# One batch's transposes moved across an output stage, one batch's value load moved behind its transposes, and a gap between batches in the event pacing

## The chip, the cores and the metric

The kernel runs on one core of a Trainium2 chip. The metric is the device time of one execution in microseconds. TensorE (PE) multiplies, VectorE (DVE) and ScalarE (ACT) move and combine data between PSUM and SBUF, GpSimd (POOL) issues most loads, and SyncE (SP) issues the DMA transposes and half of the output stores. Each engine works through its own instructions in order and waits on semaphores.

## The reference

```python
# q, k, v: (8, 12, 448, 64) float32
scores = scale * np.matmul(q, k.transpose(0, 1, 3, 2))
attn = np.maximum(scores, 0.0) ** 2 / S
attn_out = np.matmul(attn, v)
x = attn_out.transpose(0, 2, 1, 3).reshape(B * S, H * D)     # (3584, 768)
gate = np.maximum(x @ w_gate, 0.0)                           # (3584, 1536)
val = x @ w_val
return gate * val @ w_out                                    # (3584, 768)
```

Attention with a squared ReLU in the place of the softmax is followed by a gated feed-forward network over all 3584 tokens. The result is float32; the kernel computes in bfloat16 with float32 sums.

## The kernel before

**Stages.** The loop `for b in range(1, B - 1)` (line 762) has six turns, called parts here. In part b, TensorE runs the gate and value projections of batch b-1 (twelve units, `gv_units`, each of twelve steps of four matmuls) and, woven between these steps, the attention of batch b and of batches after it. After parts 2 and 4 an output stage runs for two batches (`out_pair`, by a scheme of seven block products instead of eight, with sums of blocks made on DVE by `half_sums`, line 349, and adds at line 399). After part 6 come the projections and the output of the last two batches, outside of the loop.

**Events.** Work woven in is a list of events `(unit, step, function)`. `spread` (line 702) emits all events up to a place before the step at that place, so this list is the program order on every engine. A score tile (`scores_event`, `tile_of`, `relu2`) is four matmuls, a ReLU on ACT out of PSUM (line 232) and a square on DVE into `attn` (line 233). A values event (`values_event`, `values`) is 28 matmuls over seven score tiles, an evacuation on ACT and DVE (lines 266 and 267), and two copies between partition halves on DVE (line 261). At the end of a unit ACT makes `g_sb` (line 320) and DVE the product `hT` (line 321).

**Pacing.** From batch 4 on, the attention is one stream over four batches (`stream`), of which part 4 takes batch 4 and seven tiles of batch 5, part 5 the rest of batch 5 and fourteen tiles of batch 6, part 6 the rest. `paced` (line 740) lays the events of a part out over its steps in proportion to gaps between kinds of events. The batch is the first field of each event there.

**From a load to a tile.** For batches from 2 on, k and q go through one pair of buffers (`kn_b[0]`, `qn_b[0]`). `load_qk` and `load_v` issue DMAs from POOL (line 116). `regroup(b, t, h)` copies half of k (t = 0) or q (t = 1) on DVE into `kr` or `qr` (line 180). `transpose_grouped(b, t, h)` then issues two DMA transposes from SP into `T_b[b % 2]` (line 188), shown as `kqT`. `turned` (line 722) makes the four pieces of a batch into events, a regrouping and its transposes together; the halves of one piece are five steps apart, and the first place given is k's, the second q's. Score tiles of the batch read `T_b`. A tile needs the whole of q and a part of k.

**Holds.** `hold(b)` (line 688) makes POOL copy one element that the last transposes of batch b write, for k and for q; what POOL issues after it comes no earlier than these transposes' landing. `hold_unit(b, mf)` (line 684) does the same for one `hT` product.

**Where the work stands before.** In part 4, k and q of batch 5 have been issued in the part before; its values are issued at unit 0, step 4, its pieces stand at (2, 1) and (3, 1), then POOL holds for them and loads k and q of batch 6. Batch 6's pieces stand at (9, 6) and (10, 6). The output stage of batches 2 and 3 follows. In part 5, at (2, 1), POOL holds for a unit of batch 4, loads the values of batch 6, holds for batch 6's transposes, and loads k and q of batch 7, whose pieces stand at (7, 6) and (8, 6). The values event of batch 5 that ends part 4 stands at (11, 5).

Of the kernel before, what the change touches and what calls it, by code (L numbers as in the profile page):

```python
# [16 lines left out]
def kernel(  # L17
# [33 lines left out]
    NC = S // 64  # L51
# [16 lines left out]
    def pin(ins):  # L68
        return tc.keep_in_program_order(ins)
# [45 lines left out]
    def dma_in(o, i):  # L115
        pin(nc.gpsimd.dma_start(out=o, in_=i))  # L116
# [13 lines left out]
    def load_nat(dst, src, b, h0, h1):  # L130
        lo = src[b, h0:h1, 0:256, :].rearrange("h (j i) d -> j h i d", i=4)
        hi = src[b, h0:h1, 256:448, :].rearrange("h (j i) d -> j h i d", i=3)
        dma_in(dst[0:64, h0:h1, :, :], lo)
        dma_in(dst[64:128, h0:h1, 0:3, :], hi)

    def natural(b):

        return b if b < NB else 0

    def load_qk(b, h0=0, h1=H):  # L140
        load_nat(kn_b[natural(b)], k, b, h0, h1)
        load_nat(qn_b[natural(b)], q, b, h0, h1)

    def load_v(b):
        for c, p in HALVES:
            if b == 0:
                src = v[b].rearrange("(g c h) s d -> c h g s d", c=2, h=2)[c]
                dst = v_b[b % NB][p].rearrange("p (g h) i d -> p h g i d", h=2)
                parts = [(dst[:, h2], src[h2]) for h2 in range(2)]
            else:  # L150
                parts = [(v_b[b % NB][p], v[b, c * HP:c * HP + HP])]
            for dst, src in parts:
                dma_in(dst[:, :, 0:4, :], src[:, 0:256, :].rearrange("g (j i) d -> j g i d", i=4))
                dma_in(dst[:, :, 4:7, :], src[:, 256:448, :].rearrange("g (j i) d -> j g i d", i=3))
# [21 lines left out]
    def regroup(b, t, h):  # L176

        nat, grp = ((kn_b[natural(b)], kr), (qn_b[natural(b)], qr))[t]
        i = slice(2 * h, 2 * h + 2)
        pin(nc.vector.tensor_copy(grp.rearrange("p i (h d) -> p i h d", d=D)[:, i],  # L180
                                  nat.rearrange("p h i d -> p i h d")[:, i]))

    def transpose_grouped(b, t, h):

        grp = (kr, qr)[t]
        for i in (2 * h, 2 * h + 1):
            r = 128 if i < 3 else 64
            pin(nc.sync.dma_start_transpose(out=T_b[b % NB][:, t, :, i * 128:i * 128 + r], in_=grp[0:r, i, :]))
# [108 lines left out]
    def new_x(b):  # L297
        x = [xpool.tile([128, HP, S], BF16, name=f"x{n}") for n in range(2)]
        x_of[b] = [quads(t) for t in x]
        return x  # L300
# [284 lines left out]
    def gv_units(b):  # L585
        b0 = b - b % 2
        if b == b0:
            hT_of[b0] = hpool.tile([128, KF, 2 * S], BF16, name="hT")
        return [gv_unit(b, mf, BEGUN, rotation((BEGUN_IN[mf],))) if b == 0 and mf < len(BEGUN_IN) else
                gv_unit(b, mf, BEGUN if mf == 0 else STRAIGHT, acc) for mf in range(KF)]  # L590
# [85 lines left out]
    def values_event(b, qd):  # L676
        return lambda: (values_by_parity if b >= B - 2 else values)(b, qd, sc_later())

    def transposes_event(b, qd):
        return lambda: transpose_quad(b, qd)  # L680
# [3 lines left out]
    def hold_unit(b, mf):  # L684

        pin(nc.gpsimd.tensor_copy(flag[:, 2:3], hT_of[b - b % 2][:, mf, b % 2 * S:b % 2 * S + 1]))

    def hold(b):

        for t in range(2):  # L690
            pin(nc.gpsimd.tensor_copy(flag[:, t:t + 1], T_b[b % NB][:, t, HP - 1, S - 1:S]))  # L691
# [26 lines left out]
    def step(units, u, n, k):  # L718
        at = len(units[-1]) * u + n + k
        return at // len(units[-1]), at % len(units[-1])  # L720

    def turned(b, units, *at):

        def piece(t, h):
            regroup(b, t, h)
            transpose_grouped(b, t, h)
        return [(*step(units, u, n, 5 * h), lambda t=t, h=h: piece(t, h)) for t, (u, n) in enumerate(at) for h in range(2)]

    def stream(b0, b1):

        e = []
        for b in range(b0, b1):
            for n in range(NT):
                if n % NC == 2 and (b, n) != (b0, 2):
                    vb, qd = (b, n // NC - 1) if n > NC else (b - 1, NQ - 1)
                    e.append((b, n, values_event(vb, qd), NC))
                e.append((b, n, scores_event(b, n), 1))
        return e

    def paced(units, first, behind, events):  # L740

        at = [(u, n) for u in range(len(units)) for n in range(len(units[u]))][first:behind]
        gaps = [{(1, 1): 1, (1, NC): 0.35, (NC, 1): 0.75}[a[3], b[3]] for a, b in zip(events, events[1:])]
        gap = len(at) / (sum(gaps) + 1)
        places, due = [], gap / 2
        for (*_, e, _), g in zip(events, gaps + [0]):
            u, n = at[int(due)]
            places.append((u, n, e))
            due += g * gap
        return places  # L750
# [5 lines left out]
    units = gv_units(0)  # L756
# [5 lines left out]
    for b in range(1, B - 1):  # L762
        if b < B - 3:
            new_x(b)
        units = units[2:] if b == 1 else gv_units(b - 1)
        last = len(units) - 1
        if b < B - 4:
            first, behind = {1: (24, 105), 2: (40, 132)}.get(b, (0, 132))
            events = paced(units, first, behind, stream(b, b + 1))
            events.append((last, 8 if b == 1 else 5, values_event(b, NQ - 1)))  # L770
        else:
            todo = [e for e in attention if e[:2] <= ENDS[b]]
            del attention[:len(todo)]
            if b == B - 4:
                begun = flat(kn_b[1], 4, S)
                x_of[b + 1] = [[begun[:, 2 * e:2 * e + 2, :]] for e in range(2)]
                del attention[[e[3] for e in attention].index(NC)]
            events = paced(units, 0, 144 if b == B - 3 else 132, todo)
            if b != B - 3:
                events.append((last, 5, values_event(*((b + 1, 0) if b == B - 4 else (B - 1, NQ - 1)))))  # L780
        if b == 1:
            events += [(1, 2 + 4 * qd, transposes_event(1, qd)) for qd in range(NQ)]
            events += turned(2, units, (last - 3, 7), (last - 2, 7))
            events += [(last, 2, lambda: (hold(2), load_v(2), load_wo(), load_qk(3)))]
        elif b == 2:
            events += [(1, 1, lambda: load_v(3))]
            events += [(last - 5 + 2 * n, 6, lambda n=n: weight_sums(2 * n)) for n in range(2)]
            events += [(last - 1 + t, 3 + 5 * h, lambda t=t, h=h: regroup(3, t, h)) for t in range(2) for h in range(2)]
            events += [(last, 10, lambda: [transpose_grouped(3, t, h) for t in range(2) for h in range(2)])]
        elif b == 3:  # L790
            events += [(2, 1, lambda: (hold_unit(2, 1), hold(3), load_qk(4), load_v(4)))]
            events += turned(4, units, (6, 1), (7, 1)) + [(8, 4, lambda: (hold(4), load_qk(5)))]
        elif b == 4:
            events += [(0, 4, lambda: load_v(5))]
            events += turned(5, units, (2, 1), (3, 1)) + [(5, 4, lambda: (hold(5), load_qk(6)))]
            events += turned(6, units, (last - 2, 6), (last - 1, 6))
        elif b == 5:
            events += [(2, 1, lambda: (hold_unit(4, 1), load_v(6), hold(6), load_qk(7)))]
            events += turned(7, units, (last - 4, 6), (last - 3, 6))
            later = [xpool.tile([128, HP, S], BF16, name=f"x{n}") for n in range(2)]  # L800
            x_of[b] = [x_of[b][e] + quads(later[e])[1:] for e in range(2)]
            x_of[B - 2] = [quads(t)[:1] for t in later]
        elif b == 6:
            events += [(3, 1, lambda: (hold(7), load_v(7)))]
            new = [xpool.tile([128, HP, S], BF16, name=f"x{n}") for n in range(2)]
            x_of[b] = [x_of[b][e] + quads(new[e])[1:] for e in range(2)]
            x_of[B - 1] = [quads(flat(t, HP, S)) for t in (kr, qr)]
        spread(units, events)
        if b == 2:
            out_pair(0, flat(kn_b[1], KH, S), [lambda: weight_sums(1), lambda: weight_sums(3)])  # L810
        elif b == 4:
            out_pair(2, flat(v_b[0], KH, S))
# [48 lines left out]
```

## Time and profile before

| | |
|---|---|
| three runs, us | 401.11, 402.35, 404.22 |
| median, us | 402.35 |
| profiled execution: its own time, us | 403.33 |
| profiled execution: span of its instructions, us | 401.6 |
| PE busy, us (share of the span) | 389.9 (97%) |
| DVE busy, us | 302.9 (75%) |
| ACT busy, us | 243.6 (61%) |
| POOL busy, us | 96.3 (24%) |
| part 4, from its first step to the output stage | 160.3 to 200.6 us |
| output stage of batches 2 and 3 | 200.6 to 224.7 us |
| part 5 | 224.7 to 261.3 us |
| part 6 | 261.3 to 300.5 us |

All times in the profile count from the start of the span in the profiled execution. In the timelines a line gives the start, the length, the engine, the line of the kernel, the operation, what it writes and reads, how many instructions are merged, and in brackets how long the engine was idle before it and what ended that. In the windows view, each engine has its busy time and its number of instructions, and then come the granted clock of TensorE, the DMA engines' busy share and GB/s.

### The profile page before, as it was taken

The numbers are of one execution on the slowest core, as the hardware profiler recorded it, in microseconds if no ns is written. First come the engines' busy times: TensorE is split into PE (matmuls) and PEld (weight loads), VectorE is DVE, ScalarE is ACT, GpSimd is POOL, SyncE is SP. The second block draws the span as 40 slices with busy tenths as digits, with TensorE's granted clock in tenths as the row PEclk, the third lists the DMA queues.
The fourth block names the chain that finished last, engine by engine and source line by source line (L and its number), as shares of the span: only waits on it lengthen the run. The fifth ranks groups of instructions, "written<-read, shape, count | busy, mean of one in ns | idle before, by whom it ended". The sixth has DMA issues, their size and how long they took to land.

```text
span 401.6 us, 16574 instructions
## 1 busy us (share of the span) xinstructions
PE 389.9 (97%) x7376; PEld 290.5 (72%) x7376; DVE 302.9 (75%) x530; ACT 243.6 (61%) x358; POOL 96.3 (24%) x168
## 2 busy tenths in 40 slices
PE   7899999999999999999899999999999999999995
PEld 3466779978776666679677666988887766777664
DVE  4985896699944696887781478988889969997922
ACT  3962994787334776988533588899883234344231
POOL 7933300810213600503031360020003230000223
PEclk9999999999999999999999999999999999999999
DMA  9999998999836894997963588770002350000036
GB/s 151 168 196 197 196 191 97 155 205 179 135 83 179 108 163 82 149 154 86 171 110 80 160 108 103 122 89 4 4 2 52 77 153 3 2 3 3 20 83 177
DMA packets 90872, 44.17 MB, mean 110 GB/s; under 512 B 55424, under 2 KB 89792, under 8 KB 90800
## 3 DMA queue, kind: packets, MB, share of 16 engines
q0 software_dynamic: 51264, 28.83, 50.5%
q1 hardware_dynamic: 39104, 13.99, 19.8%
q8 instruction: 57, 0.93, 1.0%
q10 hardware_dynamic: 432, 0.30, 0.3%
q14 instruction: 15, 0.12, 0.1%
HBM read 47.19 MB, written 11.01 MB: 145 GB/s over the span
## 4 chain that ended last, share of the span: by engine, by line
PE 86%; DMA 5%; DVE 5%; issue 1%; ACT 1%; POOL 1%; ACTq 0%; DVEq 0%; POOLq 0%
PE ps L72 85%; DMA qn<-in_q_dram 5%; DVE attn L233 2%; ACT r_sb L232 1%; PE ps L208 1%; DVE kqT L209 1%; POOL kn L116 1%; POOL qn L116 0%; DVE x L267 0%; DVE hT L321 0%; DVE r_sb L630 0%; DVE x L653 0%; PE ps L217 0%; DVE x L261 0%; ACT g_sb L320 0%
## 5 line engine op out<-in xcount | busy, mean ns | idle before, releaser
L72 PE MATMUL ps<-x,gv 64*64 64x448 bf16 x3408 | 198.4, 349 | 1.2 <-DVE hT L321 0.9
L72 PEld LDWEIGHTS <-gv 64*64 64x64 bf16 x4032 | 150.5, 107 | 44.5 <-issue 2.9
L232 ACT ACTIVATE r_sb<-ps 128x896 bf16<-128x896 f32 x167 | 149.0, 933 | 17.7 <-PE ps L72 15.0
L233 DVE TENSOR_TENSOR attn<-r_sb 128x896 bf16<-128x896 bf16 x167 | 101.9, 622 | 29.2 <-ACT r_sb L232 22.0
L409 POOL DMA_DIRECT2D out_dram<-attn x63 | 33.1, 530 | 170.0 <-DVE attn L399 134.6
L72 PE MATMUL ps<-kqT 64*64 64x448 bf16 x672 | 68.6, 351 | 3.4 <-ACT r_sb L232 2.6
L72 PEld LDWEIGHTS <-hT 128*64 128x64 bf16 x1056 | 55.9, 110 | 20.9 <-issue 1.4
L395 ACT ACTIVATE attn<-ps 128x384 f32<-128x384 f32 (+1 forms) x64 | 28.8, 450 | 64.3 <-PE ps L72 63.3
L72 PE MATMUL ps<-wo,hT 128*64 128x384 bf16 (+1 forms) x720 | 54.3, 306 | 0.0
L321 DVE TENSOR_TENSOR hT<-ps,g_sb 128x448 bf16<-128x448 f32 x72 | 44.5, 619 | 8.3 <-ACT g_sb L320 7.5
L320 ACT ACTIVATE g_sb<-ps 128x448 bf16<-128x448 f32 x72 | 39.2, 546 | 17.3 <-PE ps L72 17.1
L399 DVE TENSOR_TENSOR attn<-ps,attn 128x384 f32<-128x384 f32 (+1 forms) x48 | 22.8, 503 | 33.0 <-ACT attn L395 18.4
L72 PEld LDWEIGHTS <-vn 64*64 64x64 bf16 (+1 forms) x888 | 35.8, 107 | 12.3 <-issue 2.3
L72 PEld LDWEIGHTS <-kqT 64*64 64x64 bf16 x672 | 28.3, 106 | 14.1 <-issue 6.0
L72 PE MATMUL ps<-attn,vn 64*64 64x448 bf16 x672 | 37.8, 350 | 0.7 <-DVE attn L233 0.7
L528 ACT ACTIVATE kqT<-ps 128x896 f32<-128x896 f32 x18 | 16.5, 918 | 25.0 <-PE ps L72 25.0
L116 POOL DMA_DIRECT2D vn<-in_v_dram x36 | 23.7, 678 | 17.8 <-PE ps L72 5.8
L72 PE MATMUL ps<-o_ring,hT 128*64 128x384 bf16 (+1 forms) x336 | 26.0, 306 | 0.0
L532 DVE TENSOR_TENSOR kqT<-ps,kqT 128x896 f32<-128x896 f32 x18 | 19.5, 1086 | 5.9 <-PE ps L72 4.2
L691 POOL COPY flag<-kqT 128x1 bf16<-128x1 bf16 x12 | 2.2, 197 | 89.7 <-DMA kqT<-kr 48.3
L116 POOL DMA_DIRECT2D qn<-in_q_dram x20 | 14.8, 762 | 1.3 <-POOLq L845 0.8
L261 DVE COPY x<-x 64x896 bf16<-64x896 bf16 x34 | 13.5, 397 | 1.8
(101 smaller groups left out, 288.5 us busy)
## 6 DMA issues: line engine op xcount, KB each, us to landing
out_dram<-attn POOLq DMA_DIRECT2D x48, 96.0 KB, 2.3
out_dram<-attn SPq DMA_DIRECT2D x48, 96.0 KB, 2.6
kn<-in_k_dram POOLq DMA_DIRECT2D x7, 384.0 KB, 6.8
qn<-in_q_dram POOLq DMA_DIRECT2D x7, 384.0 KB, 9.2
vn<-in_v_dram POOLq DMA_DIRECT2D x14, 192.0 KB, 8.8
gv<-in_moe_w_gate_dram POOLq DMA_DIRECT2D x6, 384.0 KB, 11.6
gv<-in_moe_w_val_dram POOLq DMA_DIRECT2D x6, 384.0 KB, 11.8
wo<-in_moe_w_out_dram POOLq DMA_DIRECT2D x2, 1152.0 KB, 13.7
```

The source lines that it names most:

```text
L72: pin(nc.tensor.matmul(o, lhsT=l, rhs=r, start=start, stop=stop, skip_group_check=True))
L116: pin(nc.gpsimd.dma_start(out=o, in_=i))
L232: pin(nc.scalar.activation(r, src, AF.Relu))
L233: pin(nc.vector.tensor_tensor(dst, r, r, ALU.mult))
L261: pin(nc.vector.tensor_copy(x1[p], x0[other]))
L320: pin(nc.scalar.activation(g_sb, o[0], AF.Relu, scale=float(out_scale)))
L321: pin(nc.vector.tensor_tensor(hT[:, mf, col:col + S], o[1], g_sb, ALU.mult))
L395: pin(nc.scalar.activation(out_of(t, r, c), bank(P, t), AF.Copy))
L399: pin(nc.vector.tensor_tensor(o, bank(Q, t), o, ALU.add))
L409: pin(engines[c].dma_start(out=rows[:, c0:c1, :], in_=src))
L528: pin(nc.scalar.activation(held(n, j), both(PQ[n][0]), AF.Copy))
L532: pin(nc.vector.tensor_tensor(k, both(PQ[n][1]), k, ALU.add))
```

## The change

In part 4, batch 5's pieces come one unit later, its values are loaded after the hold for its transposes and ahead of k and q of batch 6, and batch 6 is only regrouped, in the last two units; its eight DMA transposes are issued at the beginning of part 5, which in program order is behind the output stage. In part 5, the hold on a unit is gone, the hold for batch 6 comes ahead of its values, and this and batch 7's pieces stand later. In `paced`, the gap between two events of different batches is larger by one; only the streams of parts 4, 5 and 6 hold such a pair.

```diff
     def paced(units, first, behind, events):
 
         at = [(u, n) for u in range(len(units)) for n in range(len(units[u]))][first:behind]
-        gaps = [{(1, 1): 1, (1, NC): 0.35, (NC, 1): 0.75}[a[3], b[3]] for a, b in zip(events, events[1:])]
+        gaps = [{(1, 1): 1, (1, NC): 0.35, (NC, 1): 0.75}[a[3], b[3]] + (a[0] != b[0]) for a, b in zip(events, events[1:])]
         gap = len(at) / (sum(gaps) + 1)
...
         elif b == 4:
-            events += [(0, 4, lambda: load_v(5))]
-            events += turned(5, units, (2, 1), (3, 1)) + [(5, 4, lambda: (hold(5), load_qk(6)))]
-            events += turned(6, units, (last - 2, 6), (last - 1, 6))
+            events += turned(5, units, (3, 1), (4, 1)) + [(5, 4, lambda: (hold(5), load_v(5), load_qk(6)))]
+            events += [(last - 1 + t, 3 + 5 * h, lambda t=t, h=h: regroup(6, t, h)) for t in range(2) for h in range(2)]
         elif b == 5:
-            events += [(2, 1, lambda: (hold_unit(4, 1), load_v(6), hold(6), load_qk(7)))]
-            events += turned(7, units, (last - 4, 6), (last - 3, 6))
+            events += [(0, 0, lambda: [transpose_grouped(6, t, h) for t in range(2) for h in range(2)])]
+            events += [(3, 1, lambda: (hold(6), load_v(6), load_qk(7)))]
+            events += turned(7, units, (last - 3, 11), (last - 2, 11))
             later = [xpool.tile([128, HP, S], BF16, name=f"x{n}") for n in range(2)]
```

`last` is 11, the number of the last unit.

## Prediction, before the result

> **What bounds the kernel now.** I read the page first: TensorE (PE) is busy for 97% of the span, so only PE time counts. The windows view of the three parts that the edits touch comes next (part 4 is the one with b = 4, and so on):
>
> ```profile
> PE 389.9 (97%) x7376; PEld 290.5 (72%) x7376; DVE 302.9 (75%) x530; ACT 243.6 (61%) x358; POOL 96.3 (24%) x168
> ```
>
> ```profile
> 160.30:200.60 40.30, 38.50 (x800) 30.25 (x792) 32.07 (x60) 32.11 (x44) 9.00 (x14) 1.00 1.15 140
> 224.70:261.30 36.60, 36.60 (x776) 26.20 (x778) 29.43 (x54) 31.15 (x43) 7.42 (x14) 1.00 0.74 114
> 261.30:300.50 39.20, 39.20 (x833) 33.16 (x824) 33.72 (x60) 34.79 (x51) 2.83 (x5) 1.00 0.19 25
> ```
>
> The first figure after the stretch is its length, the second PE's busy time; the clock is 1.00 throughout. Now count the work. One step of a unit and one score tile are each one pass of four matmuls, and a values event is seven passes. Part 5 has 144 steps, 28 tiles and 3 values events: 193 passes in 36.6 us, 0.190 us each. Part 6 has 207 in 39.2 us, 0.189 us each. Part 4 has 200 and should take 37.9 us; it takes 40.3. So parts 5 and 6 are dense, and part 4 loses 2.4 us. That is all that these edits can win, 0.6% of the kernel.
>
> Where the 2.4 us go is in the timelines of PE and of VectorE (DVE):
>
> ```profile
> 194.22 0.95 PE L72 MATMUL ps<-x,gv 64*64 64x448 bf16 x14
> 196.03 1.13 PE L72 MATMUL ps<-x,gv 64*64 64x448 bf16 x18 [0.87 <-DVE hT L321]
> 196.82 1.48 PE L72 MATMUL ps<-attn,vn 64*64 64x448 bf16 x24
> 199.00 0.38 PE L72 MATMUL ps<-attn,vn 64*64 64x448 bf16 x4 [0.70 <-DVE attn L233]
> ```
>
> ```profile
> 193.88 0.56 DVE L180 COPY kr<-kn 128x1536 bf16<-128x1536 bf16 x1 [1.71 <-issue]
> ...
> 197.85 0.56 DVE L180 COPY qr<-qn 128x1536 bf16<-128x1536 bf16 x1 [0.81 <-issue]
> 198.33 0.62 DVE L233 TENSOR_TENSOR attn<-r_sb 128x896 bf16<-128x896 bf16 x1
> ```
>
> DVE works in order. At 193.88 and 197.85 it starts regrouping batch 6, and not before, because the loads of k and q land at 193.80 and 197.77; it reached these instructions at 191.4 and 194.7. A hT product and a square for attn are queued behind, and PE stands still for them twice, about 1.1 and 0.9 us beyond its pass time. The rest, some 0.4 us, is the same thing at 173.2, with q of batch 5 (landed 171.40). Why batch 6 is loaded so late stands in the timelines of GpSimd (POOL) and of SyncE (SP):
>
> ```profile
> 163.54 2.69 POOL L116 DMA_DIRECT2D vn<-in_v_dram  x4
> 180.62 0.19 POOL L691 COPY flag<-kqT 128x1 bf16<-128x1 bf16 x1 [14.40 <-DMA kqT<-kr]
> 186.03 0.20 POOL L691 COPY flag<-kqT 128x1 bf16<-128x1 bf16 x1 [5.22 <-DMA kqT<-qr]
> 186.54 1.50 POOL L116 DMA_DIRECT2D kn<-in_k_dram  x2 [0.32 <-DVE attn L233]
> ```
>
> ```profile
> 168.58 7.66 SPq L188 DMA_TRANSPOSE kqT<-kr  x4
> 176.76 7.93 SPq L188 DMA_TRANSPOSE kqT<-qr  x4
> 194.51 5.39 SPq L188 DMA_TRANSPOSE kqT<-kr  x4
> 199.99 6.14 SPq L188 DMA_TRANSPOSE kqT<-qr  x4
> ...
> 250.18 5.95 SPq L188 DMA_TRANSPOSE kqT<-kr  x4
> 256.22 6.05 SPq L188 DMA_TRANSPOSE kqT<-qr  x4
> ```
>
> The hold makes POOL wait until the eight transposes of batch 5 have landed, at 185.91. They took 17.3 us from the first issue, beside the values of batch 5, which landed between 172.4 and 176.7. The sets for batches 6 and 7 took 12.8 and 13.2 us.
>
> **The change, part by part.** Places are turned into times by the number of passes ahead of them, at 0.189 us, from 160.3 (part 4) and 224.7 (part 5).
>
> (1) *Batch 5's regrouping, one unit later.* The first copy moves from unit 2 to unit 3, step 1: 45 passes, 168.8; the hT product of unit 2 on DVE is ahead of it (its g_sb ran 169.1 to 169.6 on ScalarE, the product takes 0.62), so it runs at about 170.1 and SP issues the first transpose at 170.6. k has landed at 167.9. The q copy moves to unit 4 (67 passes, 173.0), after 171.4, so the stop at 173 goes: -0.4 us, inside the 2.4. The four copies (0.56 each) and eight transposes are the same in number.
>
> (2) *Values of batch 5 after the hold.* The transposes then have only the tail of q beside them. I take batch 7's 13.2 us: batch 5 done at 183.8 instead of 185.91. Bounds: 12.8 (batch 6) and 17.3 (nothing gained by the move); in between lies batch 4's 15.3, three us of it beside loads. PE's first tile of batch 5 stands at pass 137, 186.2, so this term is covered by 2.4 us.
>
> [...]
>
> (3) *The loads behind it.* From the last landing to the first issue 0.63 us pass (185.91 to 186.54): 184.4. Now comes the price: four issues for v stand ahead of k and q of batch 6. The nearest row is part 5 before, same order and nothing beside it: first issue 232.75, v landed 7.7 us later, k 11.2, q 15.0. So v at 192.2 (its values event at pass 186 begins at 195.5: covered), k at 195.7, q at 199.4. That is 1.9 and 1.6 us *later* than before, in spite of (2).
>
> (4) *Batch 6's regrouping, nine steps later.* k goes to unit 10, step 3 (170 passes, 192.5), q to unit 11, step 3 (184 passes, 195.1). DVE lags about 1 us behind; it waits for k some 2 us and for q about as long. What is queued behind is another set of work. Behind k's two copies: the squares of the last two score tiles, which the last pass of the values event needs. Copy 0.5, square 0.6, copy 0.5, square 0.6: the last pass starts 2.3 us after k lands. Before, 1.64 us lay between that pass (199.00) and the first product of the output stage (200.64), and 6.9 us from there to the first product that needs the sum S2 (207.5). So that product can start at k + 10.8 = 206.5. Behind q: copy 0.5, the evacuation of the values with its exchange 1.5, copy 0.5, last hT product 0.5, then six half sums of 0.77, the last of which is needed half a product (0.5) late; it can start at q + 7.3 = 206.7. PE without any stop would be there at 207.5 - 2.4 = 205.1. The last of the three counts: 206.7 against 207.5, **-0.8 us**. Before the change the same sums ended at 206.6, 0.9 before the need; that cover is gone.
>
> (5) *Transposes of batch 6 into part 5.* They stand on SP behind the output stores of batches 2 and 3 (last issue before: 226.78, 0.55 long), so first issue 227.4 - 0.8 = 226.6, done 13.2 later at 239.8. First need: the first tile of batch 6, pass 97, 223.9 + 18.4 = 242.3. Covered by 2.5 us: 0. Of this cover the new gap gives 0.4 (pass 97 instead of 95).
>
> (6) *Part 5's loads.* The hold on a unit goes (it kept POOL for 6.0 us, off the path); the hold for batch 6 now ends at 239.8. v first issued at 240.4, landed at 248.1 (need 253.1), k of batch 7 at 251.6, q at 255.4. The copies stand at passes 142 and 163, reached at about 251.8 and 255.8: covered by 0.2 and 0.4 only. Without that cover, a stop of DVE up to 2 us still leaves PE running, as the squares of the tiles that the values need are ahead of the first copy; in part 4 stops of 2.4 and 3.1 us cost PE 2.0. Taken at 0. Batch 7's transposes end near 266; its first tile in part 6 is at 270.
>
> (7) *The gap* moves score tiles by a few steps and adds no instruction: 0.
>
> Sum: -0.8 us on a span of 401.6, so 400.8; the profiled execution, 403.33, would be 402.5. The median of the runs shown is 402.35, 1.0 lower than that execution; less 0.8 it gives **401.6 us**. A measurement of this kernel can tell about 1% from no change, 4 us.
>
> **Rivals.** All turn on when a set of transposes ends; (3) and (4) give gain = 184.6 - (end of batch 5's set).
>
> *A, the loads come in time:* eight issues at 1.21 and a last landing after 2.3 (the shortest of the rows) make 12.0 us, 182.6, and 1.9 us gained, near the ceiling of 2.4. For it: no values beside the set. Against: every set seen had longer issues of about 2 us in it. Time 400.4.
>
> *B, slower: v in the queue ahead of q.* If batch 5's set takes over 14.0 us, the values placed in front push q of batch 6 beyond 199.9 and the output stage waits for its sums longer than all the stops of before. At batch 4's 15.3: +1.3 us, time 403.7; at 17.3, +3.3. For it: four of the six sets took 13.5 us or more, though with loads or stores beside them. Against: the two sets with least beside them. [...]
>
> *C, slower: batch 6's set behind the stores.* It decides from 15.7 us of length on, since PE then waits at pass 97 one for one, and the loads of batch 7 shift by as much. The set for batch 3, beside loads and stores, took 15.8; batch 5's 17.3 would cost 1.6: 403.2 with the rest as forecast.
>
> **How the numbers follow.** Forecast (0 to 1.4 us gained) 0.43, A 0.23, B 0.19, C 0.11, anything else 0.04. The likeliest gives 401.6; its own range is 400.9 to 402.4. Adding A down to the ceiling and B and C up to 17.3 gives gains of 2.4 to losses of 3.3 us, 400.0 to 405.7; the last us of the upper end needs the worst row, and the runs shown lie 3.1 apart, so I give 399.7 to 404.4. A gain of 4 us is beyond the ceiling: faster 0.03. A loss of 4 needs B and C together or what I don't see: 0.06. Within 1%: 0.91.
>
> **What would show it.** Right: no values load before 183 in part 4; batch 5's set in 13 us; batch 6's k and q landing near 195.7 and 199.4 and DVE still waiting at L180 for both; PE's wait now in front of the S2 products or of the last values pass; parts 5 and 6 as dense as before. Wrong: part 4 without a stop (A), S2 products after 207.5 (B), a PE wait on transposes in part 5 (C).

## The result and the profile after

The change makes the kernel slower: 407.81 us (median of 6 runs, 407.14 to 408.83) against 402.13 before, a ratio of 1.0124 with a 95% interval of 1.0100 to 1.0148. The forecast was 401.6. The profiled execution took 408.24 us, its span is 406.5 against 401.6. (Ratios here and below are made from undisturbed runs alone, which leaves out four of the twelve runs of e3, so they can differ from those of the medians.)

The windows view of PE, cut where PE's work changes; after each stretch its length, PE's busy time with the number of matmuls, the granted clock, the DMA share and GB/s:

```profile
160.40:196.50 36.10, 36.10 (x764) 1.00 0.88 121
196.50:199.60 3.10, 0.91 (x19) 1.00 1.38 173
199.60:203.00 3.40, 3.40 (x36) 0.50 0.04 4
203.00:226.40 23.40, 23.40 (x330) 1.00 0.34 86
226.40:254.00 27.60, 27.60 (x588) 1.00 0.79 121
254.00:264.00 10.00, 7.24 (x147) 1.00 1.20 161
264.00:305.90 41.90, 41.90 (x882) 1.00 0.28 37
```

Three places lose. At the end of part 4, PE is idle for 2.2 of 3.1 us. Then the granted clock is 0.50 for 3.4 us: in PE's timeline the last 28 matmuls of part 4 take 2.56 us, where they took 1.52, and the first 96 of the output stage 7.63, where they took 7.03. And part 5, dense before, is idle for 2.8 us of 10 near its end. (Parts 4 and 5 now begin at 160.4 and 226.4.)

The DVE timeline after, around batch 6's copies (L180, in part 4) and batch 7's (in part 5):

```profile
196.93 0.56 DVE L180 COPY kr<-kn 128x1536 bf16<-128x1536 bf16 x1 [2.99 <-DMA kn<-in_k_dram]
...
200.67 0.56 DVE L180 COPY qr<-qn 128x1536 bf16<-128x1536 bf16 x1 [1.10 <-issue]
...
257.96 0.56 DVE L180 COPY kr<-kn 128x1536 bf16<-128x1536 bf16 x1 [3.06 <-DMA kn<-in_k_dram]
258.44 0.62 DVE L321 TENSOR_TENSOR hT<-ps,g_sb 128x448 bf16<-128x448 f32 x1
...
262.53 0.56 DVE L180 COPY qr<-qn 128x1536 bf16<-128x1536 bf16 x1
```

The waits for batch 6 in part 4 have not gone (k landed at 196.85, q at 200.59, against 193.80 and 197.77), and there is a new one of 3.1 us for k of batch 7, whose q landed only at 261.47. Before, DVE came to the first copy of batch 7 without a wait:

```profile
249.56 0.56 DVE L180 COPY kr<-kn 128x1536 bf16<-128x1536 bf16 x1
```

PE's timeline after names what it waited for, first the squares behind batch 6's k, then what is queued behind batch 7's copies:

```profile
198.08 0.38 PE L72 MATMUL ps<-attn,vn 64*64 64x448 bf16 x4 [1.57 <-DVE attn L233]
199.08 0.38 PE L72 MATMUL ps<-attn,vn 64*64 64x448 bf16 x4 [0.62 <-DVE attn L233]
199.27 2.56 PE L72 MATMUL ps<-x,gv 64*64 64x448 bf16 x28
201.76 7.63 PE L72 MATMUL ps<-wo,hT 128*64 128x384 bf16 x96
...
259.11 0.38 PE L72 MATMUL ps<-x,gv 64*64 64x448 bf16 x2 [1.29 <-DVE hT L321]
261.83 0.38 PE L72 MATMUL ps<-kqT 64*64 64x448 bf16 x2 [1.20 <-DVE x L277]
```

The line before that answers to the 28 matmuls at half clock:

```profile
199.19 1.52 PE L72 MATMUL ps<-x,gv 64*64 64x448 bf16 x28
```

Why the loads are late stands in the timelines of SP and of POOL:

```profile
170.82 6.20 SPq L188 DMA_TRANSPOSE kqT<-kr  x4
177.54 6.32 SPq L188 DMA_TRANSPOSE kqT<-qr  x4
218.35 10.70 SPq L409 DMA_DIRECT2D out_dram<-attn  x16
229.15 6.46 SPq L188 DMA_TRANSPOSE kqT<-kr  x4
235.66 6.03 SPq L188 DMA_TRANSPOSE kqT<-qr  x4
```

```profile
185.75 1.32 POOL L116 DMA_DIRECT2D vn<-in_v_dram  x2 [0.33 <-issue]
187.54 1.32 POOL L116 DMA_DIRECT2D vn<-in_v_dram  x2 [0.47 <-issue]
188.84 1.53 POOL L116 DMA_DIRECT2D kn<-in_k_dram  x2
...
244.43 0.35 POOL L691 COPY flag<-kqT 128x1 bf16<-128x1 bf16 x1 [7.42 <-DMA kqT<-qr]
244.98 2.68 POOL L116 DMA_DIRECT2D vn<-in_v_dram  x4 [0.21 <-issue]
247.61 1.55 POOL L116 DMA_DIRECT2D kn<-in_k_dram  x2
```

In part 4, the values stand ahead of k and q. In part 5 everything is in a row: stores, batch 6's transposes (first issue 229.15, last landing 244.31), the hold, the values, then batch 7's k, issued at 247.61 where before it was 235.6.

In the spans: 1.7 us are lost up to the beginning of part 5 (226.4 against 224.7), 3.6 us in parts 5 and 6 (79.5 against 75.9), and the rest of the kernel takes 0.4 less, together the 4.9 us.

### The profile page after: what moved, and what is told of

Its sections match the earlier page's. It is cut to its first block, busy times and chain, and to the rows that moved or that the text cites. A ratio compares the mean times of both kernels' runs of the same rounds, so it can differ in the third digit from the quotient of the medians.

```text
span 406.5 us, 16576 instructions
## 1 busy us (share of the span) xinstructions
PE 391.7 (96%) x7376; PEld 275.9 (68%) x7376; DVE 303.6 (75%) x530; ACT 244.0 (60%) x358; POOL 96.6 (24%) x167
## 4 chain that ended last, share of the span: by engine, by line
PE 83%; DMA 7%; DVE 5%; issue 2%; POOL 1%; ACT 1%; SPq 0%; DVEq 0%; POOLq 0%; ACTq 0%
PE ps L72 82%; DMA qn<-in_q_dram 6%; DVE attn L233 2%; DMA kqT<-qr 1%; PE ps L208 1%; POOL vn L116 1%; ACT r_sb L232 1%; DVE hT L321 1%; DVE kqT L209 1%; POOL qn L116 0%; DVE r_sb L630 0%; DVE x L653 0%; DVE kr L180 0%; ACT x L276 0%; POOL kn L116 0%
## 5 line engine op out<-in xcount | busy, mean ns | idle before, releaser
L72 PEld LDWEIGHTS <-gv 64*64 64x64 bf16 x4032 | 139.5, 107 | 57.8 <-issue 4.5
L232 ACT ACTIVATE r_sb<-ps 128x896 bf16<-128x896 f32 x167 | 148.5, 933 | 20.6 <-PE ps L72 18.7
L233 DVE TENSOR_TENSOR attn<-r_sb 128x896 bf16<-128x896 bf16 x167 | 102.0, 622 | 30.5 <-ACT r_sb L232 24.7
L72 PE MATMUL ps<-kqT 64*64 64x448 bf16 x672 | 67.6, 351 | 4.3 <-ACT r_sb L232 2.6
L399 DVE TENSOR_TENSOR attn<-ps,attn 128x384 f32<-128x384 f32 (+1 forms) x48 | 22.8, 502 | 33.0 <-ACT attn L395 18.4
L72 PEld LDWEIGHTS <-vn 64*64 64x64 bf16 (+1 forms) x888 | 34.3, 107 | 15.4 <-issue 4.1
L72 PE MATMUL ps<-attn,vn 64*64 64x448 bf16 x672 | 37.7, 350 | 2.2 <-DVE attn L233 2.2
L72 PEld LDWEIGHTS <-kqT 64*64 64x64 bf16 x672 | 26.3, 106 | 16.8 <-issue 7.0
L528 ACT ACTIVATE kqT<-ps 128x896 f32<-128x896 f32 x18 | 16.5, 918 | 25.0 <-PE ps L72 25.0
L72 PE MATMUL ps<-kn,gv 64*64 64x448 bf16 x192 | 16.1, 349 | 0.0
L261 DVE COPY x<-x 64x896 bf16<-64x896 bf16 x34 | 14.4, 424 | 1.8
## 6 DMA issues: line engine op xcount, KB each, us to landing
gv<-in_moe_w_val_dram POOLq DMA_DIRECT2D x6, 384.0 KB, 12.2
```

Of the source, the lines that this page charges most:

```text
L72: pin(nc.tensor.matmul(o, lhsT=l, rhs=r, start=start, stop=stop, skip_group_check=True))
L232: pin(nc.scalar.activation(r, src, AF.Relu))
L233: pin(nc.vector.tensor_tensor(dst, r, r, ALU.mult))
L261: pin(nc.vector.tensor_copy(x1[p], x0[other]))
L399: pin(nc.vector.tensor_tensor(o, bank(Q, t), o, ALU.add))
L528: pin(nc.scalar.activation(held(n, j), both(PQ[n][0]), AF.Copy))
```

## The experiments

In this section "+x" is a time from the start of part 4 or of part 5 in the profile of that kernel, so that kernels can be compared. Times of runs are compared with the kernel before on the same chip, at 402.4 to 403.1 us.

**The pacing gap taken out** (e1).

```diff
-        gaps = [{...}[a[3], b[3]] + (a[0] != b[0]) for a, b in zip(events, events[1:])]
+        gaps = [{...}[a[3], b[3]] for a, b in zip(events, events[1:])]
```

> The change whole, but without the larger gap between batches in the pacing. Theory (late loads): the 5.7 us that the change cost come from VectorE waiting at L180 for batch 6's q in part 4 and for batch 7's k and q in part 5; the gap moves tiles by a few steps only. So 407 to 408 us, and the waits at L180 stay (about 3 us for batch 7's k in part 5). Rival (pacing): the gap squeezes the other events and stops PE; without it the time falls to 404 or less. A third possibility: without the gap the first tile of batch 6 stands two passes (0.4 us) earlier and PE waits for its transposes, 0.1 to 0.5 us more.

407.13 us, ratio 1.0102 (1.0073 to 1.0131): the loss stays, and the gap is not its cause. The profiled execution was the quickest of the six (405.30 us; the others took 406.92 to 408.79), so it is not typical, and it differed from the expectation: batch 6's transposes took 13.0 us instead of 15.2, batch 7's k landed at +28.7 instead of +31.5, VectorE waited 0.5 us for it and parts 5 and 6 lost 0.6 us only, while in part 4 PE's stop before the values was 2.8 us long. Two executions of nearly the same program, then, put the loss in different places. Of the 2.8 us by which k landed earlier in part 5, 2.2 are the shorter set of transposes; the loads behind it took 12.2 us to k instead of 12.9.

**Part 4 alone** (e2).

```diff
-            events += [(0, 4, lambda: load_v(5))]
-            events += turned(5, units, (2, 1), (3, 1)) + [(5, 4, lambda: (hold(5), load_qk(6)))]
-            events += turned(6, units, (last - 2, 6), (last - 1, 6))
+            events += turned(5, units, (3, 1), (4, 1)) + [(5, 4, lambda: (hold(5), load_v(5), load_qk(6)))]
+            events += turned(6, units, (last - 1, 3), (last, 3))
```

> The kernel before with the change's part 4 alone: batch 5's pieces a unit later, its values behind the hold, batch 6 regrouped in the last two units, but its transposes issued right with the regrouping, and part 5 and the pacing as before. Theory: batch 6's q lands near 200.6 as in the changed kernel, the products with S2 start 0.4 (at full clock) to 1.7 us later than before, part 5 loses nothing: 402.5 to 404. Rival (all of the loss is made in part 4 and only shows later): 406 or more.

404.75 us, ratio 1.0036 (1.0012 to 1.0060); parts 5 and 6 take 75.9 us as before. q of batch 6 lands at +40.2, as in the change, and the first product with S2 starts at +47.3, by the prediction's chain at +47.5 (before +47.2, in the change +48.8). The windows view of this kernel from the start of its output stage:

```profile
201.00:204.40 3.40, 3.40 (x52) 1.00 0.74 155
```

PE's stops before it were 1.39 and 0.62 us long, but the clock (the 1.00) stayed full. In these two profiles, then, the change's 1.5 us more at S2 are the half-clock stretch; the 28 and 96 matmuls above took 1.6 us longer in it.

The other executions of e2 are not all like the profiled one. For each the mean granted clock is on record, and one stretch of 3.4 us at half clock lowers it by 0.004 (half of 3.4 us in a span of some 404; the profiled execution of the change, with one stretch in its span, has 0.996). Five have 0.999 or 1.000 and took 401.95 to 404.23 us; seven have 0.993 or 0.996 and took 404.41 to 406.28. So e2's 404.75 holds half-clock stretches too, by these means, and the median of the five, 402.94, is close to the kernel before (402.66 on that chip). Where they lay is not on record, since only one execution was profiled.

**Part 5 alone** (e3, and e8 the same kernel again).

```diff
-            events += turned(6, units, (last - 2, 6), (last - 1, 6))
+            events += [(last - 2 + t, 6 + 5 * h, lambda t=t, h=h: regroup(6, t, h)) for t in range(2) for h in range(2)]
         elif b == 5:
-            events += [(2, 1, lambda: (hold_unit(4, 1), load_v(6), hold(6), load_qk(7)))]
-            events += turned(7, units, (last - 4, 6), (last - 3, 6))
+            events += [(0, 0, lambda: [transpose_grouped(6, t, h) for t in range(2) for h in range(2)])]
+            events += [(3, 1, lambda: (hold(6), load_v(6), load_qk(7)))]
+            events += turned(7, units, (last - 3, 11), (last - 2, 11))
```

> The kernel before with the change's part 5 alone: batch 6 regrouped where it was, its transposes at the beginning of part 5, then hold, values, k and q of batch 7, whose pieces stand later; pacing without the larger gap. Theory: part 5 loses about 3.3 us to VectorE's wait for batch 7's k and q, part 4 loses its 2.4 as before: 405 to 406. Rival (part 5's loss comes only because part 4 ended late): the chain from the stores to batch 7's k is tied to part 5's own start, so this would show as 402 to 403.

> The change's part 5 alone once more, since its runs fell into two groups, 399.2 to 401.0 and 403.6 to 406.3. Theory: batch 7's k is covered by a few tenths of a us, so that batch 6's set of transposes (13 to 15 us) and the loads (15 to 16.5 us) decide from run to run: two groups again, some 4 us apart. Rival (something of that chip): one group.

The first time 404.93 us (402.66 before), with four of the twelve runs at 399.2 to 401.0 and eight at 403.6 to 406.3, and a ratio that decides nothing (0.9986, 0.9946 to 1.0025), since it is made from four of each group. The second time there was one group, 403.9 to 406.8, median 404.8, ratio 1.0045 (1.0025 to 1.0065). Two groups were thus not reproduced, and what made the four quick runs is open: none of them was profiled. Both profiles show the loss: batch 6's set 15.0 and 16.0 us long, batch 7's k at +31.0 and +31.2, VectorE waiting for it for 2.4 and 1.9 us, parts 5 and 6 at 78.8 and 79.0 us instead of 75.9. Part 4 didn't end later than before (39.7 and 39.6 us against 40.3). So part 5's loss is its own. It is not all VectorE's: the first tile of batch 6 stands at +18.0 here, and it began 0.2 us after the set's last landing, 0.3 us late in e3 and 1.0 in e8. So PE seems to have waited for the set itself, though the profile names ACT as what ended these waits.

**Batch 7's pieces a unit later** (e4).

```diff
-            events += turned(7, units, (last - 3, 11), (last - 2, 11))
+            events += turned(7, units, (last - 2, 11), (last - 1, 11))
```

> The change whole, with batch 7's pieces one unit later still, at (9, 11) and (10, 11). Theory: k of batch 7 lands about 31.5 us after part 5's start, the copy is now reached at about 32, q lands at 35 and is reached at 34.5, so VectorE waits less than 1 us in all and PE gets back 2.5 to 3.3 us: 404.5 to 405.5. Rival (PE's stops in part 5 are not due to these copies): no change, 407 to 408.

404.8 us, ratio 1.0053 (1.0032 to 1.0074), as expected. k landed at +29.7 and was reached after that; VectorE doesn't wait at L180 in part 5, and parts 5 and 6 take 77.0 us. So 2.5 of the 3.6 us lost there are the meeting of late loads with early copies. The other 1.1 us have another cause, which is open: PE's only listed stop there is 0.2 us long.

**k and q of batch 7 ahead of the hold** (e5).

```diff
-            events += [(3, 1, lambda: (hold(6), load_v(6), load_qk(7)))]
+            events += [(3, 1, lambda: (load_qk(7), hold(6), load_v(6)))]
```

> The change whole, but in part 5 k and q of batch 7 are issued ahead of the hold for batch 6, the values of batch 6 behind it. Theory (serial chain: stores, batch 6's transposes, hold, values, then k and q): k and q of batch 7 now land before 250, VectorE doesn't wait at L180 in part 5, and the 3 us lost there come back, less what batch 6's transposes lose beside these loads (a set beside loads took 15 to 17 us, and PE's first tile of batch 6 stands 18.4 us after the part's start, the set begins some 3 us after it: 0 to 2 us lost): 404 to 406. Rival (it is the regrouping's place or the late transposes themselves): 407 or more.

410.71 us, ratio 1.0192 (1.0166 to 1.0217), slower than the change itself. The time falls into the rival's range, but by neither mechanism as I put it: VectorE no longer waits, while PE now stands before the first tile of batch 6. SP's timeline, and PE's from the list of its waits:

```profile
227.85 8.75 SPq L188 DMA_TRANSPOSE kqT<-kr  x4
236.65 10.11 SPq L188 DMA_TRANSPOSE kqT<-qr  x4
```

```profile
PE ps L72 <- DMA kqT<-qr: 3.7, 1, 3.7
PE ps L72 <- ACT r_sb L232: 1.2, 1, 1.2
```

Beside these loads the set took 20.7 us (+2.8 to +23.4), more than the 15 to 17 that I had expected, and the tile's place is +18.4. (The 1.2 us stop, some 2 us ahead of this tile, came with the edit too; its cause was not followed up.) After the stop of 3.7 us came 3.4 us at half clock again (249.5 to 252.9), and parts 5 and 6 took 83.3 us. With the transposes behind the output stage, the loads waited for them in the one order (k at +31.5), and in the other the set, beside the loads, was 5.5 us longer than in the change (20.7 us against 15.2).

**Batch 6's transposes back ahead of the output stage** (e9), the rest of the change kept.

```diff
-            events += [(last - 1 + t, 3 + 5 * h, lambda t=t, h=h: regroup(6, t, h)) for t in range(2) for h in range(2)]
+            events += turned(6, units, (last - 1, 3), (last, 3))
         elif b == 5:
-            events += [(0, 0, lambda: [transpose_grouped(6, t, h) for t in range(2) for h in range(2)])]
```

> The change whole, but batch 6's transposes issued right with its regrouping at the end of part 4, ahead of the output stage. Theory (part 5's loss comes from the place of these transposes behind the output stores): the hold in part 5 is over before it is reached, batch 7's k and q land before 255, VectorE doesn't wait for them, part 5 is dense; what is left is part 4's loss: 402.5 to 405. Rival (the later hold and the later pieces of batch 7 cost by themselves): 406.5 or more.

404.03 us, ratio 1.0052 (1.0023 to 1.0081). The set is over 15 us before part 5 begins, k of batch 7 lands at +12.8, and parts 5 and 6 take 76.3 us instead of 79.5. The place of the transposes is what costs in part 5.

**What costs in part 4.** Three kernels start from the one before and have batch 6's pieces at (10, 3) and (11, 3), with their transposes. They differ in batch 5's pieces and values:

```diff
-            events += turned(6, units, (last - 2, 6), (last - 1, 6))
+            events += turned(6, units, (last - 1, 3), (last, 3))
# e6: no more than this.  e10 besides:
-            events += [(0, 4, lambda: load_v(5))]
-            events += turned(5, units, (2, 1), (3, 1)) + [(5, 4, lambda: (hold(5), load_qk(6)))]
+            events += turned(5, units, (2, 1), (3, 1)) + [(5, 4, lambda: (hold(5), load_v(5), load_qk(6)))]
# e11 instead:
-            events += turned(5, units, (2, 1), (3, 1)) + [(5, 4, lambda: (hold(5), load_qk(6)))]
+            events += turned(5, units, (3, 1), (4, 1)) + [(5, 4, lambda: (hold(5), load_qk(6)))]
```

> The kernel before with one edit: batch 6's pieces nine steps later, at (10, 3) and (11, 3), transposes with them. Theory: k and q of batch 6 land at 193.8 and 197.8 as before, VectorE reaches them at 193.4 and 196.1, so it waits 0.4 and 1.7 us instead of 2.4 and 3.1, and the S2 products can start at 197.8 + 7.3 = 205.1, when PE gets there: 2 us faster than before, 400 to 401. Rival (the place of the regrouping is what costs in part 4 of the change): as slow as the kernel with the change's part 4 alone, 404 or more.

> The kernel before with batch 6's pieces at (10, 3) and (11, 3), as in e6, and batch 5's values behind the hold, batch 5's pieces at their old places. Tells apart what makes part 4 of the change slow. Theory 1 (batch 5's later pieces use up what its transposes gain without the values beside them): the set begins at 168.6, ends near 182.5, k and q of batch 6 land near 194 and 198: 400 to 401.5, as e6. Theory 2 (the values in front of k and q are the price): k and q land as late as in the change, 196.9 and 200.6: 403 to 405.

> The kernel before with batch 6's pieces at (10, 3) and (11, 3), and batch 5's pieces a unit later, its values at unit 0 as before: the other half of the change's part 4. Theory 1 (the later pieces cost): the set begins at 170.8 beside the values, ends at 186 to 188, k and q of batch 6 land at 194.5 and 198.5 or later: 400.5 to 402. Theory 2 (the values' place alone costs): as fast as e6, 400 to 401, with the set ending at 185 or before.

| kernel | batch 5's pieces | its values | its set of transposes | k, q of batch 6 landed | output stage from | time, us | ratio to before |
|---|---|---|---|---|---|---|---|
| before | unit 2 | early | +8.3 to +25.6, 17.3 us | +33.5, +37.5 | +40.3 | 402.1 (402.4 to 403.1 beside the others) | |
| e2 | unit 3 | behind hold | +10.6 to +24.5, 13.9 us | +36.3, +40.2 | +40.2 | 404.75 | 1.0036 (1.0012 to 1.0060) |
| e6 | unit 2 | early | +8.4 to +25.6, 17.2 us | +33.5, +37.7 | +38.4 | 400.62 | 0.9941 (0.9923 to 0.9959) |
| e10 | unit 2 | behind hold | +8.1 to +21.6, 13.5 us | +34.3, +37.9 | +38.7 | 401.84 | 0.9989 (0.9962 to 1.0017) |
| e11 | unit 3 | early | +10.6 to +24.7, 14.1 us | +32.8, +36.7 | +37.7 | 400.10 | 0.9941 (0.9919 to 0.9962) |

Regrouping batch 6 later, alone (e6), gains 2.4 us, as much as the prediction counted for part 4 (in its profile part 4 is 1.9 us shorter). Moving batch 5's pieces a unit later (e11) doesn't cost: its set, which runs beside the last 4 us of the values' loads where the set before ran beside 8, is 14.1 us long, the same as without them (14.3 in the change), and ends 0.9 us earlier than before. So in this pair the values' place alone costs: e2 and e11 differ in it only, and k and q land 3.5 us later in e2. That was theory 2. (Of the 4.65 us between their times a part is the half clock in seven of e2's executions.) Theory 1 has a share: with the pieces at their old place and the values behind the hold (e10), the set ends 4.0 us earlier, which pays for the values in front, and k and q land nearly as in e6. In time e10 stands between the two; its runs go from 400.3 to 405.1, and its interval includes no change (1.0). DVE still stops for batch 5's q there (1.4 us idle at 170.8).

PE in e11, part 4 first, then parts 5 and 6:

```profile
159.70:197.40 37.70, 37.70 (x802) 1.00 1.16 141
221.40:297.30 75.90, 75.90 (x1604) 1.00 0.47 68
```

Part 4 is dense, 37.7 us against 40.3: it beats both kernels.

**Batch 5's q later** (e7): e6 and

```diff
-            events += turned(5, units, (2, 1), (3, 1)) + [(5, 4, lambda: (hold(5), load_qk(6)))]
+            events += turned(5, units, (2, 1), (3, 6)) + [(5, 4, lambda: (hold(5), load_qk(6)))]
```

> As e6, and batch 5's q pieces five steps later, at (3, 6): VectorE then reaches them after q's landing at 171.4. Theory: 0.4 us more than e6, 399.7 to 400.7; SP is busy with k's transposes until 176 anyway, so batch 5's set ends no later. Rival: the set ends later by the five steps (1 us), the loads of batch 6 too, and the gain of e6 halves.

401.05 us, ratio 0.9950 (0.9932 to 0.9968), the same as e6 within the intervals. In the profile the stop at 173 is gone, PE has no other in part 4, and the set ends at +25.2, so the rival's price isn't paid; the 0.4 us don't show in the time.

## Why the prediction was wrong

*The ceiling* was right: the 2.4 us counted from passes are what e6 and e11 win. The prediction missed the span by 5.7 us (406.5 against 400.8): 2.5 up to the beginning of part 5, where it had 0.8 gained and 1.7 were lost, and 3.6 in parts 5 and 6, where it had none; the rest took 0.4 less.

*(1), batch 5's first transpose* at 170.6: it was 170.82.

*(2), its set*: 14.3 us instead of 13.2, ending at 185.11 instead of 183.8. By the prediction's own formula the 0.8 us gained become 0.5 lost. And its reason was only half of the story: e11 gets the same length by the later start, with the values' last 4 us beside it, e10 nearly the same (13.5) with the earlier start and no values beside it; one of the two edits is enough, and the change pays for both.

*(3) and (4), loads and chain*: right. From the first issue of the values k took 11.1 us and q 14.8 (11.2 and 15.0 forecast); the last values pass started 2.2 us after k (2.3); in e2 the S2 products came 0.2 us ahead of q + 7.3. This was rival B's side of the sum. What the prediction did not have is the half clock behind the stop: 1.5 us by the comparison of the two profiles of the change and e2.

*(5), batch 6's set in part 5*: first issue 2.7 us after the part's start, as forecast; 15.2 us long instead of 13.2. PE had no wait on it, but only 0.5 us of the 2.5 us of cover were left, so rival C did not come as described. In e8, with a set of 16.0 us and without the gap's 0.4 us, it seems to have come, at 1.0 us.

*(6) is the step that failed*, and it is the larger part of the miss. It had the copies covered by 0.2 and 0.4 us and took a stop of DVE behind that cover at nothing. The set was 2.0 us longer, and the loads behind it took 12.9 us to k and 16.5 to q instead of 11.2 and 15.0, so k landed at +31.5 instead of +27.7. DVE waited 3.1 us, where the prediction held up to 2 to be free, and parts 5 and 6 lost 3.6 us (2.8 of them as PE's idle time in that stretch); with a set of 13.0 us (e1) they lost 0.6, with the copies later (e4) 1.1, with the set ahead of the output stage (e9) 0.4. That up to 2 us should be free rested in part on a misreading: the "stops of 2.4 and 3.1 us" before, which cost PE 2.0, were counted from when DVE's queue began to wait, and DVE was still working then. Its idle time, the brackets of the lines in the prediction, was 1.71 and 0.81 us: 2.5 us of idle DVE had cost 2.0 us of PE, nearly one for one. The range did add a longer set, in rival C, but priced only PE's own wait for the tiles, from 15.7 us of length on. With a set of 15.0 us (e3), 2.9 us were lost, of which that wait can explain 0.3; most of the price came through DVE's queue. The 0.4 and 1.1 us of e9 and e4, where DVE does not wait for batch 7, are not explained by it.

*(7), the gap*: no effect on the time that can be told from noise, as forecast (e1).

The halves measured alone give 1.0036 and 1.0045, 0.8% together; the whole gives 1.24%. The intervals leave room for the two to agree; if the difference of 0.4% is real, its cause is open. By the mean granted clock, the profiled executions of the change, e1 and e4 (0.996 each) and e5 (0.992) have half-clock stretches and those of e2 (0.999) and e9 (1.000) have none, but such a stretch can't be named as the cause: by their mean clock seven of e2's twelve executions had such stretches too, and the one execution of the change with a mean granted clock of 1.000 took 407.19 us, among the others' 407.14 to 408.83.

An earlier issue went both ways: k of batch 7 lands 18.7 us earlier in e9 than in the change, k of batch 6 3.5 us earlier in e11 than in e2, and both are quicker. In e5 k and q of batch 7 are issued earlier too; batch 6's set beside them takes 20.7 us instead of 15.2, and e5 is the slowest of all.

## What to carry to other kernels

A chain of transfers that each wait for the one before (stores, transposes, hold, loads) must be priced with the spread of each link, not with one of its best rows (batch 6's set in part 5 took 13.0 to 16.0 us in the change, e1, e3 and e8); a cover of a few tenths of a microsecond at its end is no cover. A copy placed ahead of its data cost what stood behind it on its engine (in the change DVE waited 3.1 us at batch 7's k, and PE was idle for 2.8 us in that stretch), so the cheapest edit was to move the copy later, not the transfers (2.4 us gained in e6). When a stop is priced, the engine's idle time counts, not the wait of its queue, which began here while the engine still worked (before, DVE was idle for 1.71 and 0.81 us in queue waits of 2.4 and 3.1). If two edits remove the same delay, take the one that puts nothing in front of what is needed next.

## What the runs showed of the hardware

The granted clock of PE was 0.50 for 3.4 us at a time after some stops and not after others. In the change it was 0.50 from 199.6 to 203.0, after stops of 1.57 and 0.62 us, and in e5 from 249.5 to 252.9, after one of 3.7 us. It stayed at 1.00 after stops of 1.39 and 0.62 us in e2, and after stops of 1.29 and 1.20 us in part 5 of the change. What decides is not shown by these runs.

A set of eight DMA transposes, the same for each batch, took 12.8 to 17.3 us in the profiles of the kernel before and of the change, and 20.7 in e5, beside loads of k and q that were issued ahead of it.
